# Decoding the last two matrices in the later two passes, in the buffers of h; the tail's buffers laid out anew

## The chip, the cores and the metric

The kernel runs on one core of one Trainium2 chip. The time is device microseconds (us) of one execution. Engines: TensorE (PE, its weight loads PEld), VectorE (DVE), ScalarE (ACT), GpSimd (POOL) and SyncE (SP), which issues the DMA transfers. Each engine works through its own instructions in order.

## What is computed

Three blocks follow each other on 2304 tokens (4 batches of 576) of width 512. All weights are inputs; `w_in` and `w_out` are 64-bit floats that the kernel turns into 32-bit ones itself ("decoding"), since it takes them as raw words.

```python
x = block_causal_attention(q, k, v)          # 4 x 8 heads, 576 x 64, blocks of 64
P = sinkhorn(exp(x @ w_gate), 8 rounds)      # 2304 x 8
out = 0
for e in range(8):                           # all experts, weighted by P
    out += P[:, e:e + 1] * (relu(x @ w1[e]) @ w2[e])
h = out @ w_in                               # 2304 x 1024
solu = h * softmax(h)
ln = layernorm(solu) * g_ln
return ln @ w_out                            # 2304 x 512
```

## The kernel before, in words

Every 32-bit product is made of three products of a high and a low part, so each operand is split: ScalarE casts the high part, GpSimd or VectorE subtracts it to get the low part (`split_weights`, lines 526 to 529).

**Expert layers.** Expert 0 runs between the pieces of attention. Experts 1 to 7 are 14 "units" (half an expert each, u = 2 to 15) and go over the tokens in three passes of two blocks of 384. The first layer uses seven products instead of eight (`first_layer`, L798 to L800 in `product`); VectorE forms the sums between them (`plus`, L810).

- Pass 0 (tokens 0 to 767) also makes the factors of all weights: `first_factors` and `second_weights` split them on ScalarE and GpSimd and write them to DRAM (`fd`). The second layer is plain (`second_layer`, L953 to L955), and VectorE adds each product times its gate (L959): six accumulations in a unit.
- Passes 1 and 2 read the factors back (`W<-fd`, a ring of 20 tiles in pool `wr`, 14 tiles in a unit). VectorE weights h with the gate (L852) into tiles of pool `hb` (8 tiles); `steps` forms the seven sums and splits of h: ScalarE casts (L859), GpSimd subtracts (L860) and makes differences (`minus`, L863; one of the four on VectorE). The second layer has 14 products a unit, one unit behind the first layer, and VectorE accumulates them (L907). `finish_pass` joins the sums at a pass's end and writes rows to DRAM (`rd`).

**Decoding.** `decode` (L536) handles half a row block of `w_in` or `w_out`: a 256 KB load, seven VectorE operations on 128x256 (L548 to L566; an eighth for `w_out`, L568), the split by ScalarE (L528) and GpSimd (L529), and a store to DRAM (`wd`). There are 32 of them. Two tiles of 4 KB a partition in a pool of their own, `wdp`, hold the words and the result. `late_decode(n)` issues those due at step n; the list `when` asks for 6 in pass 0 and 26 in passes 1 and 2.

**Tail.** After pass 2, for each of 18 row blocks: `early` loads x and transposes or copies it, `front` multiplies by `w_in` into two double banks (pool `big`) and normalises, `turn` transposes, `back` multiplies by `w_out`. `early` for two row blocks is issued ahead of `finish_pass(2)`, the others two steps ahead of their `front`.

**What sets the order.** The code names the work in one sequence; a scheduler puts each engine's instructions in order, by priority (place in the sequence) and by when buffers and inputs are free in its own estimate. Work whose buffers are free can stand earlier on an engine than the source has it. A tile waits for the release of what lay in its place, also across pools that take turns in one address range (`left` and `right` ends of the memory).

Of the kernel before, what the change touches and what calls it, by code (L numbers as in the profile page):

```python
# [19 lines left out]
P = 128  # L20
# [7 lines left out]
def build(ctx, tc, qT, kT, v, w_gate, w1, w1s, w2, w_in, w_out, g_ln, out):  # L28
# [509 lines left out]
    def decode(i, half, src, scale=None):  # L538


        pair = wdp.tile([P, 2, 512], F32R, tag="wd", name="w64")
        raw = pair[:, 0, :].bitcast(U32)
# [26 lines left out]
        t = pair[:, 1, :].rearrange("p (s n) -> p s n", s=2)  # L569
# [451 lines left out]
    l1p = lctx.enter_context(tc.tile_pool(name="l1p", bufs=6, space=PSUM, side="right"))  # L1021
    rctx = ExitStack()
    xcp = rctx.enter_context(tc.tile_pool(name="xcp", bufs=1, side="right"))
    xraw = rctx.enter_context(tc.tile_pool(name="xraw", bufs=1, side="right"))
    wdp = rctx.enter_context(tc.tile_pool(name="wdp", bufs=2, side="right"))
    wr = rctx.enter_context(tc.tile_pool(name="wr", bufs=20, side="right"))
    sctx = ExitStack()
    sml = sctx.enter_context(tc.tile_pool(name="sml", bufs=4, side="right"))
    stg2 = sctx.enter_context(tc.tile_pool(name="stg2", bufs=2, side="right"))
    jnk = sctx.enter_context(tc.tile_pool(name="jnk", bufs=1, side="right"))  # L1030
# [42 lines left out]
    when = sorted([*range(8, 27), *range(30, 42), 36])  # L1073
# [8 lines left out]
    for u in range(2, 16):  # L1082
        hs = {}
        first_layer(W, X, plain_hidden(hs))
        if u < 15:
            W, nws = first_factors(u + 1, raws[0]), second_weights(u + 1, raws[1])
            if u < 14:
                raws = fetch_first(u + 2), fetch_second(u + 2)
        else:
            X = {}  # L1090
            run(spread_x(1, X))
            W = load_factors(2, 0)
        late_decode(u - 2)
        if u == 4:
            gate_table()
        second_layer(u, 0, ws, hs)
        ws = nws
# [7 lines left out]
    hb = ectx.enter_context(tc.tile_pool(name="hb", bufs=8, side="left"))  # L1105
# [3 lines left out]
    for n, (p, u) in enumerate([*work, (3, 2)]):  # L1109
        if n < len(work):  # L1110
# [5 lines left out]
            late_decode(n + 14)  # L1116
# [16 lines left out]
    xin = ctx.enter_context(tc.tile_pool(name="xin", bufs=2, side="right"))  # L1133
    w2p = ctx.enter_context(tc.tile_pool(name="w2p", bufs=8, side="right"))
    wi = [[load_decoded(wip, 2 * dc + f) for f in range(2)] for dc in range(4)]
    early0 = [xin.tile([P, DM], F32, tag="x", name="xin") for t in range(2)]
    for t in range(2):
        nc.sync.dma_start(early0[t], adram[:, t * DM : t * DM + DM])
    def early(t):
        x2 = w2p.tile([P, 2, 4, P], F32R, tag="w", name="x2")  # L1140
        if t < 2:
# [3 lines left out]
        if t < 6:  # L1145
            if t > 1:
# [11 lines left out]
    xs = [early(t) for t in range(2)]  # L1158
# [5 lines left out]
    wop = ctx.enter_context(tc.tile_pool(name="wop", bufs=8, side="left"))  # L1164
    wo = [load_decoded(wop, 8 + c) for c in range(8)]


    mp = ctx.enter_context(tc.tile_pool(name="mp", bufs=3, side="left"))
# [70 lines left out]
    for i in range(NT + 4):  # L1239
        if i + 2 < NT:  # L1240
# [52 lines left out]
```

## Time and profile before

| what | value |
|---|---|
| median of 3 runs | 1988.7 us (1988.07 to 1994.13) |
| the profiled execution | 1991.78 us, its span 1990.0 us |
| busy share of the span: PE, DVE, ACT, POOL | 93%, 75%, 43%, 55% |
| DMA | 300.47 MB, mean 151 GB/s |
| mean granted clock of TensorE | 0.973 |

The span runs from the first to the last instruction; a busy share over all of it mixes stages that have different limits. The granted clock is 1.00 at 2.4 GHz and 0.5 at 1.2 GHz; a value between is a mean over time at either.

### The profile page before, as it was taken

How to read it: one execution, taken by the hardware profiler on the slowest of the kernel's cores; microseconds unless marked ns; L12 is line 12 of the kernel's file. 1: busy time of each engine (PE TensorE's matmuls, PEld its weight loads, DVE VectorE, ACT ScalarE, POOL GpSimd, SP SyncE). 2: the span in 40 equal slices, each digit the busy share in tenths (PEclk: the TensorE clock that was granted, in tenths of full speed). 3: DMA queues.
4: the chain of work that ended last, by engine and by line, in shares of the span. 5: the costliest groups of instructions: out<-in, count | busy, mean ns of one | idle time of the engine just before them, and what ended most of it. 6: DMA issues, size and time to landing. Idle time of an engine off the chain costs nothing.

```text
span 1990.0 us, 31023 instructions
## 1 busy us (share of the span) xinstructions
PE 1843.5 (93%) x10548; PEld 1229.7 (62%) x10548; DVE 1501.5 (75%) x3295; ACT 849.2 (43%) x1639; POOL 1086.0 (55%) x914
## 2 busy tenths in 40 slices
PE   5799999887888888989999999999899999989999
PEld 4688988785443444445566666665566666668887
DVE  6878777678998999777657766789577667778774
ACT  5676656564554555565242222232322222224332
POOL 7665646256564555575285556667765566631000
PEclk8999999998899999999999999999999999989999
DMA  8665554344665656555554554546445445541100
GB/s 228 158 173 151 158 148 125 139 139 157 216 214 172 216 180 200 192 196 172 162 148 145 143 144 140 146 142 187 145 142 145 142 140 147 166 173 43 45 31 32
DMA packets 191710, 300.47 MB, mean 151 GB/s; under 512 B 19760, under 2 KB 77760, under 8 KB 189632
## 3 DMA queue, kind: packets, MB, share of 16 engines
q1 hardware_dynamic: 191552, 298.49, 49.8%
q8 instruction: 84, 1.38, 0.3%
q14 instruction: 74, 0.61, 0.1%
HBM read 192.96 MB, written 77.14 MB: 136 GB/s over the span
## 4 chain that ended last, share of the span: by engine, by line
PE 51%; DVE 10%; DMA 3%; issue 2%; POOL 2%; ACT 1%; SPq 0%; POOLq 0%; ACTq 0%; DVEq 0%
PE yps L800 6%; PE yps L799 6%; PE yps L798 6%; PE psb L798 3%; PE psb L799 3%; PE psb L800 3%; PE psc L798 2%; PE psc L799 2%; PE psc L800 2%; PE psa L800 2%; PE psa L799 2%; PE psa L798 2%; PE ops L1230 2%; PE ops L1231 2%; PE ops L1232 2%
## 5 line engine op out<-in xcount | busy, mean ns | idle before, releaser
L860 POOL TENSOR_TENSOR hf<-hb,hf 128x768 f16<-128x768 f32 x196 | 324.0, 1667 | 242.9 <-ACT hf L859 242.8
L859 ACT CAST hf<-hb 128x768 f16<-128x768 f32 x196 | 159.8, 831 | 419.2 <-POOL hb L863 200.3
L799 PEld LDWEIGHTS <-W 128*128 128x128 f16 x1960 | 193.6, 99 | 170.1 <-issue 45.4
L907 DVE SCALAR_TENSOR_TENSOR acc<-yps,rscw,acc 128x384 f32<-128x384 f32 x364 | 220.7, 615 | 85.5 <-PE yps L800 84.0
L798 PEld LDWEIGHTS <-W 128*128 128x128 f16 x1960 | 193.8, 99 | 141.7 <-ACT W L528 10.2
L800 PEld LDWEIGHTS <-W 128*128 128x128 f16 x1960 | 194.0, 99 | 132.2 <-issue 4.9
L798 PE MATMUL yps<-hf,W 128*128 128x384 f16 x784 | 255.9, 327 | 4.8 <-ACT acc L905 4.5
L799 PE MATMUL yps<-hf,W 128*128 128x384 f16 x784 | 256.2, 327 | 0.0
L800 PE MATMUL yps<-hf,W 128*128 128x384 f16 x784 | 255.5, 327 | 0.0
L798 PE MATMUL psb<-X,W 128*128 128x384 f16 x504 | 166.7, 331 | 27.7 <-DVE u L810 16.5
L863 POOL TENSOR_TENSOR hb<-hb 128x768 f32<-128x768 f32 x84 | 153.4, 1827 | 24.3 <-DVE hb L852 22.3
L799 PE MATMUL psb<-X,W 128*128 128x384 f16 x504 | 166.5, 330 | 0.0
L800 PE MATMUL psb<-X,W 128*128 128x384 f16 x504 | 166.0, 330 | 0.0
L810 DVE TENSOR_TENSOR u<-psb,r 128x384 f32<-128x384 f32 x168 | 92.3, 551 | 88.2 <-PE psb L800 80.4
L953 PE MATMUL yps<-w,h 128*128 128x512 f16 x336 | 132.3, 394 | 27.4 <-DVE acc L959 24.3
L529 POOL TENSOR_TENSOR w<-raw,w 128x512 f16<-128x512 f32 (+1 forms) x96 | 119.9, 1266 | 46.0 <-ACT w L528 45.6
L245 POOL TENSOR_SCALAR e<-e,sv 128x128 f32<-128x128 f32 (+2 forms) x144 | 82.8, 577 | 98.4 <-DVE sv L241 37.7
L529 POOL TENSOR_TENSOR W<-raw,W 128x512 f16<-128x512 f32 x84 | 106.4, 1282 | 51.0 <-ACT W L528 47.1
L954 PE MATMUL yps<-w,h 128*128 128x512 f16 x336 | 132.2, 394 | 0.0
L955 PE MATMUL yps<-w,h 128*128 128x512 f16 x336 | 131.3, 391 | 0.0
L1214 POOL TENSOR_SCALAR lh<-ln 128x1024 f16<-128x1024 f32 x18 | 18.8, 1046 | 188.7 <-DVE sm L1186 86.1
L798 PE MATMUL psa<-X,W 128*128 128x384 f16 x336 | 111.7, 332 | 6.5 <-ACT W L528 4.9
(258 smaller groups left out, 4728.5 us busy)
## 6 DMA issues: line engine op xcount, KB each, us to landing
W<-fd SPq DMA_DIRECT2D x392, 256.0 KB, 2.7
fd<-W SPq DMA_DIRECT2D x154, 256.0 KB, 2.2
raw<-in_w1s SPq DMA_DIRECT2D x14, 1024.0 KB, 5.9
raw<-in_w SPq DMA_DIRECT2D x14, 1024.0 KB, 6.2
fd<-w SPq DMA_DIRECT2D x84, 128.0 KB, 2.2
raw<-in_w SPq DMA_DIRECT2D x40, 256.0 KB, 3.4
kh<-khigh SPq DMA_DIRECT2D x64, 144.0 KB, 2.6
kl<-kraw SPq DMA_DIRECT2D x64, 144.0 KB, 2.7
```

The lines of the kernel that those rows point to most:

```text
L529: nc.gpsimd.tensor_tensor(t[:, 1, :], raw, full(t[:, 0, :]), op=ALU.subtract)
L798: nc.tensor.matmul(ps, wh, xl, start=start and kc == 0, stop=False, skip_group_check=True)
L799: nc.tensor.matmul(ps, wh, xh, start=False, stop=False, skip_group_check=True)
L800: nc.tensor.matmul(ps, wl, xh, start=False, stop=stop and kc == 1, skip_group_check=True)
L810: nc.vector.tensor_tensor(to, bank[g, a], tmp[g, "r1" if a == "b" else name[1:]], op=ALU.add)
L859: nc.scalar.copy(hi, a)
L860: nc.gpsimd.tensor_tensor(lo, a, hi, op=ALU.subtract)
L863: eng.tensor_tensor(o, a, b, op=ALU.subtract)
L907: nc.vector.scalar_tensor_tensor(a, ps, r, a, op0=ALU.mult, op1=ALU.add)
L953: nc.tensor.matmul(ps, hl, ws[c][:, 0, :], start=c == 0, stop=False)
L954: nc.tensor.matmul(ps, hh, ws[c][:, 1, :], start=False, stop=False)
L955: nc.tensor.matmul(ps, hh, ws[c][:, 0, :], start=False, stop=c == 3)
```

## The change

The two tiles of a decoding now come from `hb`, the ring of h's tiles in passes 1 and 2, which grows from 8 to 10 tiles; the pool `wdp` goes. The list `when` now holds only steps of passes 1 and 2 (n = 0 to 26, with two decodings at 4, 8, 18, 22 and 24), and pass 0 no longer calls `late_decode`.

In the tail, x has four tiles (`xin`) below the pools of the passes, the first four row blocks are loaded into them once pass 0's sums are in DRAM, and `early` for three row blocks is issued ahead of `finish_pass(2)`. Its results have a pool of their own (`x2p`), the small buffers (`mp`) lie on the other side, and a tile without use (`gap`) sets the distance between pools.

```diff
     def decode(i, half, src, scale=None):
-        pair = wdp.tile([P, 2, 512], F32R, tag="wd", name="w64")
-        raw = pair[:, 0, :].bitcast(U32)
+        raw, t = (hb.tile([P, 2, BLK], F32, tag="hb", name=f"w{i}") for i in ("64", "32"))
+        raw, t = (a.rearrange("p k n -> p (k n)")[:, 0:512] for a in (raw, t))
+        raw = raw.bitcast(U32)
...
-        t = pair[:, 1, :].rearrange("p (s n) -> p s n", s=2)
+        t = t.bitcast(F32R).rearrange("p (s n) -> p s n", s=2)
         split_weights(t, f)
...
+    xin = ctx.enter_context(tc.tile_pool(name="xin", bufs=4, side="right"))
     rctx = ExitStack()
...
-    wdp = rctx.enter_context(tc.tile_pool(name="wdp", bufs=2, side="right"))
+    rctx.enter_context(tc.tile_pool(name="gap", bufs=1, side="right")).tile([P, 1792], F32, name="gap")
+    sml = rctx.enter_context(tc.tile_pool(name="sml", bufs=4, side="right"))
+    jnk = rctx.enter_context(tc.tile_pool(name="jnk", bufs=1, side="right"))
     wr = rctx.enter_context(tc.tile_pool(name="wr", bufs=20, side="right"))
...
-    when = sorted([*range(8, 27), *range(30, 42), 36])
+    when = sorted([*range(27), 4, 8, 18, 22, 24])
...
-        late_decode(u - 2)
         if u == 4:
             gate_table()
...
-    hb = ectx.enter_context(tc.tile_pool(name="hb", bufs=8, side="left"))
+    hb = ectx.enter_context(tc.tile_pool(name="hb", bufs=10, side="left"))
...
-            late_decode(n + 14)
+            late_decode(n)
...
-    xin = ctx.enter_context(tc.tile_pool(name="xin", bufs=2, side="right"))
-    w2p = ctx.enter_context(tc.tile_pool(name="w2p", bufs=8, side="right"))
+    x2p = ctx.enter_context(tc.tile_pool(name="x2p", bufs=3, side="right"))
+    mp = ctx.enter_context(tc.tile_pool(name="mp", bufs=3, side="right"))
...
-    early0 = [xin.tile([P, DM], F32, tag="x", name="xin") for t in range(2)]
-    for t in range(2):
+    early0 = [xin.tile([P, DM], F32, tag="x", name="xin") for t in range(4)]
+    for t in range(4):
         nc.sync.dma_start(early0[t], adram[:, t * DM : t * DM + DM])
...
-    xs = [early(t) for t in range(2)]
+    xs = [early(t) for t in range(3)]
     finish_pass(2)
...
+    w2p = ctx.enter_context(tc.tile_pool(name="w2p", bufs=6, side="left"))
...
-    mp = ctx.enter_context(tc.tile_pool(name="mp", bufs=3, side="left"))
...
-        if i + 2 < NT:
+        if 0 < i < NT - 2:
             xs.append(early(order[i + 2]))
```

Most lines behind the first edit move by one, so L959 of before is L960 of the change.

VectorE in pass 0, unit u = 5, from the first accumulation (`acc<-yps`) on. Here `psc`, `psb` are sums of the first layer, `raw` and `s` the factors, `h` the low parts of h, `a`, `b`, `f` (and `w`) a decoding. Before:

```order
L959 SCALAR_TENSOR_TENSOR acc<-yps,prw,acc 128x512 x2
L810 TENSOR_TENSOR psc<-psc,u_7152 128x384
L560 ISA a_13152<-a_13152,b_13153 128x512
L751 TENSOR_TENSOR raw<-s_7261,raw 128x512
L784 TENSOR_TENSOR s_7312<-raw_7024 128x512
L810 TENSOR_TENSOR psc<-psc,u_7161 128x384
L562 TENSOR_SCALAR b_13153<-w_13150 128x256
L566 SCALAR_TENSOR_TENSOR f_13160<-b_13153,a_13152 128x256
L959 SCALAR_TENSOR_TENSOR acc<-yps,prw,acc 128x512
L757 TENSOR_TENSOR raw<-raw 128x512
L841 SCALAR_TENSOR_TENSOR h<-psb,h 128x384
L548 TENSOR_SCALAR a_13457<-w_13455 128x256
```

The same place in the change, to the sixth accumulation of the unit:

```order
L960 SCALAR_TENSOR_TENSOR acc<-yps,prw,acc 128x512
L752 TENSOR_TENSOR raw<-s_7265,raw 128x512
L785 TENSOR_TENSOR s_7316<-raw_7028 128x512
L960 SCALAR_TENSOR_TENSOR acc<-yps,prw,acc 128x512
L811 TENSOR_TENSOR psc<-psc,u_7156 128x384
L811 TENSOR_TENSOR psc<-psc,u_7165 128x384
L758 TENSOR_TENSOR raw<-raw 128x512
L842 SCALAR_TENSOR_TENSOR h<-psb,h 128x384
L960 SCALAR_TENSOR_TENSOR acc<-yps,prw,acc 128x512
L842 SCALAR_TENSOR_TENSOR h<-psb,h 128x384
L842 SCALAR_TENSOR_TENSOR h<-psc,h 128x384 x2
L960 SCALAR_TENSOR_TENSOR acc<-yps,prw,acc 128x512 x3
```

Before, operations of two decodings stand among the accumulations of this unit; in the change there is none in any unit of pass 0.

VectorE in a steady unit of pass 1, the accumulations of the second layer. Before:

```order
L907 SCALAR_TENSOR_TENSOR acc<-yps,rscw,acc 128x384
L852 SCALAR_TENSOR_TENSOR hb<-psc,pb 128x384
L907 SCALAR_TENSOR_TENSOR acc<-yps,rscw,acc 128x384
L907 SCALAR_TENSOR_TENSOR acc_10396<-yps,rscw,acc_10396 128x384 x6
L907 SCALAR_TENSOR_TENSOR acc<-yps,rscw,acc 128x384 x4
L863 TENSOR_TENSOR hb<-hb 128x768
```

In the change, a unit with one decoding:

```order
L908 SCALAR_TENSOR_TENSOR acc<-yps,rscw,acc 128x384 x2
L549 TENSOR_SCALAR a_10940<-w_10937 128x256
L558 TENSOR_SCALAR b_10941<-w_10937 128x256
L908 SCALAR_TENSOR_TENSOR acc_10308<-yps,rscw,acc_10308 128x384
L552 SCALAR_TENSOR_TENSOR a_10940<-w_10937,a_10940 128x256
L908 SCALAR_TENSOR_TENSOR acc_10308<-yps,rscw,acc_10308 128x384
L555 SCALAR_TENSOR_TENSOR a_10940<-w_10937,a_10940 128x256
L908 SCALAR_TENSOR_TENSOR acc_10308<-yps,rscw,acc_10308 128x384
L561 ISA a_10940<-a_10940,b_10941 128x512
L908 SCALAR_TENSOR_TENSOR acc_10308<-yps,rscw,acc_10308 128x384
L563 TENSOR_SCALAR b_10941<-w_10937 128x256
L567 SCALAR_TENSOR_TENSOR f_10948<-b_10941,a_10940 128x256
```

The decoding's operations stand between the accumulations, one by one; six more accumulations follow.

GpSimd in the same pass: splits (`hf`), differences (`hb`) and, in the change, the decoding's subtraction (`w<-f`). Before, one unit:

```order
L860 TENSOR_TENSOR hf<-hb,hf 128x768 x6
L863 TENSOR_TENSOR hb<-hb 128x768 x2
L860 TENSOR_TENSOR hf<-hb,hf 128x768
L863 TENSOR_TENSOR hb<-hb 128x768
L860 TENSOR_TENSOR hf<-hb,hf 128x768 x6
```

In the change:

```order
L861 TENSOR_TENSOR hf<-hb,hf 128x768 x6
L864 TENSOR_TENSOR hb<-hb 128x768
L529 TENSOR_TENSOR w_11242<-f_11252,w_11242 128x256
L864 TENSOR_TENSOR hb<-hb 128x768
L861 TENSOR_TENSOR hf<-hb,hf 128x768
L864 TENSOR_TENSOR hb<-hb 128x768
L861 TENSOR_TENSOR hf<-hb,hf 128x768 x6
```

The subtraction of the decoding stands between the first two differences of a unit.

## Rows read from the trace of the kernel before

**Rows 1.** Busy us of each engine by stretch (x instructions), granted clock, DMA share, GB/s.

```profile
459.00:811.00 352.00, 285.36 (x1392) 141.95 (x1391) 325.56 (x614) 188.81 (x314) 204.03 (x168) 0.91 0.62 199
811.00:985.00 174.00, 167.76 (x892) 87.08 (x891) 126.81 (x238) 92.17 (x150) 91.40 (x76) 1.00 0.52 170
1046.00:1319.00 273.00, 273.00 (x1682) 164.38 (x1681) 192.43 (x331) 65.82 (x90) 167.41 (x100) 1.00 0.51 143
1319.00:1441.00 122.00, 112.72 (x670) 66.20 (x669) 97.69 (x140) 41.01 (x64) 92.21 (x53) 0.97 0.54 163
```

The columns behind the length are PE, PEld, DVE, ACT, POOL.

**Rows 2.** One line of the decoding: ns min/median/max, first and last start.

```profile
L551 DVE SCALAR_TENSOR_TENSOR a<-w,a x32: 406/418/1376, 461.4 to 808.2; 128x256 uint32<-128x256 uint32 x32
```

**Rows 3.** Groups by line, 459 to 818 us: count | busy us, mean ns | idle before.

```profile
L557 DVE TENSOR_SCALAR b<-w 128x256 uint32<-128x256 uint32 x32 | 24.7, 772 | 0.0
L551 DVE SCALAR_TENSOR_TENSOR a<-w,a 128x256 uint32<-128x256 uint32 x32 | 23.5, 735 | 0.0
L554 DVE SCALAR_TENSOR_TENSOR a<-w,a 128x256 uint32<-128x256 uint32 x32 | 22.2, 693 | 0.3
L566 DVE SCALAR_TENSOR_TENSOR f<-b,a 128x256 f32<-128x256 uint32 x32 | 20.7, 648 | 1.0
L562 DVE TENSOR_SCALAR b<-w 128x256 uint32<-128x256 uint32 x32 | 19.9, 623 | 0.3
L548 DVE TENSOR_SCALAR a<-w 128x256 uint32<-128x256 uint32 x32 | 19.9, 622 | 12.6 <-DMA w<-in_w_out 6.4 <-DMA w<-in_w_in 6.1
L560 DVE CUSTOM_DVE_ANT_0 a<-a,b 128x512 uint16<-128x512 uint16 x32 | 18.6, 582 | 0.2
L568 DVE TENSOR_SCALAR f<-f,gsc 128x256 f32<-128x256 f32 x16 | 9.3, 580 | 0.2
L529 POOL TENSOR_TENSOR w<-f,w 128x256 fp32r<-128x256 f32 x32 | 27.0, 842 | 67.6 <-ACT w L528 67.6
L528 ACT CAST w<-f 128x256 fp32r<-128x256 f32 x32 | 12.8, 400 | 51.5 <-DVE f L566 20.4 <-issue 19.2 <-DVE f L568 4.9
```

**Rows 4.** Waits of TensorE, 459 to 811 us: us in total, times, longest.

```profile
PE yps L953 <- DVE acc L959: 18.6, 13, 3.7
PE psb L798 <- DVE u L810: 15.2, 7, 6.6
PE tot L454 <- DVE acc L959: 10.5, 6, 3.4
PE psa L798 <- ACT W L528: 4.9, 3, 2.2
```

**Rows 5.** Accumulations of pass 1 by stretch: DVE busy (x instructions), clock, DMA share, GB/s.

```profile
1046.00:1319.00 273.00, 85.45 (x140) 1.00 0.51 143
```

**Rows 6.** Timeline of VectorE: start us, length us.

```profile
613.44 1.37 DVE L551 SCALAR_TENSOR_TENSOR a<-w,a 128x256 uint32<-128x256 uint32 x1
```

**Rows 7.** Timeline of GpSimd at the same time.

```profile
613.33 5.09 POOL L529 TENSOR_TENSOR w<-raw,w 128x512 f16<-128x512 f32 x4
```

**Rows 8.** Groups by line, 1046 to 1319 us.

```profile
L860 POOL TENSOR_TENSOR hf<-hb,hf 128x768 f16<-128x768 f32 x70 | 114.2, 1643 | 96.1 <-ACT hf L859 96.1
L863 POOL TENSOR_TENSOR hb<-hb 128x768 f32<-128x768 f32 x30 | 54.4, 1813 | 9.3 <-DVE hb L852 8.5
```

**Rows 9.** Timeline of VectorE at the start of the tail [idle before].

```profile
1759.04 5.38 DVE L941 SCALAR_TENSOR_TENSOR acc<-y,cpi,acc 128x768 f32<-128x768 f32 x4
...
1774.13 2.35 DVE L1181 TENSOR_REDUCE nm<-h 128x1 f32<-128x1024 f32 x2
```

**Rows 10.** Timeline of TensorE at the start of the tail.

```profile
1770.17 1.29 PE L1150 MATMUL xtp<-ident,xin 128*128 128x128 f32 x8 [2.65 <-DMA xin<-ad]
1775.47 1.94 PE L1150 MATMUL xtp<-ident,xin 128*128 128x128 f32 x8 [4.01 <-DVE nm L1181]
1778.57 0.77 PE L1177 MATMUL h<-w,x 128*128 128x512 f32 x1 [1.16 <-DVE sm L1186]
```

More of the change, by code (lines that the diff above doesn't have):

```diff
@@ L1024, in build @@
     xraw = rctx.enter_context(tc.tile_pool(name="xraw", bufs=1, side="right"))
-    wdp = rctx.enter_context(tc.tile_pool(name="wdp", bufs=2, side="right"))
+    rctx.enter_context(tc.tile_pool(name="gap", bufs=1, side="right")).tile([P, 1792], F32, name="gap")
+    sml = rctx.enter_context(tc.tile_pool(name="sml", bufs=4, side="right"))
+    jnk = rctx.enter_context(tc.tile_pool(name="jnk", bufs=1, side="right"))
     wr = rctx.enter_context(tc.tile_pool(name="wr", bufs=20, side="right"))
     sctx = ExitStack()
-    sml = sctx.enter_context(tc.tile_pool(name="sml", bufs=4, side="right"))
     stg2 = sctx.enter_context(tc.tile_pool(name="stg2", bufs=2, side="right"))
-    jnk = sctx.enter_context(tc.tile_pool(name="jnk", bufs=1, side="right"))
     ones = const.tile([P, P], F32, name="ones")
@@ L1132, in build @@
     wip = ctx.enter_context(tc.tile_pool(name="wip", bufs=8, side="right"))
-    xin = ctx.enter_context(tc.tile_pool(name="xin", bufs=2, side="right"))
-    w2p = ctx.enter_context(tc.tile_pool(name="w2p", bufs=8, side="right"))
+    x2p = ctx.enter_context(tc.tile_pool(name="x2p", bufs=3, side="right"))
+    mp = ctx.enter_context(tc.tile_pool(name="mp", bufs=3, side="right"))
     wi = [[load_decoded(wip, 2 * dc + f) for f in range(2)] for dc in range(4)]
-    early0 = [xin.tile([P, DM], F32, tag="x", name="xin") for t in range(2)]
-    for t in range(2):
+    early0 = [xin.tile([P, DM], F32, tag="x", name="xin") for t in range(4)]
+    for t in range(4):
         nc.sync.dma_start(early0[t], adram[:, t * DM : t * DM + DM])
     def early(t):
-        x2 = w2p.tile([P, 2, 4, P], F32R, tag="w", name="x2")
-        if t < 2:
+        x2 = x2p.tile([P, 2, 4, P], F32R, tag="x2", name="x2")
+        if t < 4:
             x = early0[t]
@@ L1145, in early @@
         if t < 6:
-            if t > 1:
+            if t > 3:
                 nc.sync.dma_start(x, adram[:, t * DM : t * DM + DM])
```

## The prediction

> **What bounds the kernel now.** I read the busy times by stretch first. Pass 0 of the expert layers begins near 459 us and its 14 units end at 985 us. In passes 1 and 2 TensorE is busy all the time at the full granted clock, while pass 0 falls in two halves that do the same kind of work [rows 1]. From 459 to 811 us VectorE is busy 325.56 of 352 us, and TensorE only 285.36 at a mean granted clock of 0.91. From 811 to 985 us VectorE is at 126.81 of 174 us, and TensorE at 167.76 at 1.00. The reader is to see that the bound changes inside one pass, at 811 us.
>
> What stops at 811 us is the decoding. The 32 decodings (seven VectorE operations each, eight for `w_out`) all start between 461 and 808 us [rows 2], although the source asks for 26 of them in passes 1 and 2: the scheduler pulled them forward, since nothing but the two buffers of `wdp` held them back. They cost 24.7 + 23.5 + 22.2 + 20.7 + 19.9 + 19.9 + 18.6 + 9.3 = 158.8 us of VectorE, 4.96 us each [rows 3]. That is nearly half of its busy time in that stretch.
>
> The waits of TensorE there are for VectorE: 18.6 us for a bank that the accumulation has not emptied, 15.2 us for `plus`, 10.5 us ahead of `total` [rows 4]. These rows say that in the first half of pass 0 taking VectorE work away is worth TensorE time, which a share of busy time over the whole span (75% for VectorE) would hide.
>
> **What the change moves, and what it is worth in pass 0.** A decoding now needs two tiles of `hb`, a pool that is opened after pass 0. So none can be pulled forward, and the order shows the accumulations of unit 5 with no decoding among them, where before pieces of two stood. I take pass 0 without decodings to run as its second half did. That half did 892 matmuls in 174 us, 5.13 per us; at that pace the 1392 matmuls of the first half [rows 1] take 271.5 us instead of 352, a gain of 80.5 us. I count by matmuls and not by units, since at 811 us TensorE stands in the middle of later units' first layers. I take off 6 us for what the second half does not have: the gate table in unit 4 and the first unit, which waits for its weights on ScalarE (waits on `W` L528 are 4.9 us in [rows 4], and I leave most of them in place). So the term is **-74 us**. Its bounds: at most 90 us, if the pace were that of no stop at all (167.76 us for the 892 give 262 for the 1392); at least half of it, 37 us, if another chain takes over (first rival). VectorE itself would not: its 325.56 us less the 158.8 are 167 us in 271.
>
> **What the decodings cost in passes 1 and 2.** A steady unit there has 14 accumulations; 140 in 273 us make ten units of 27.3 us [rows 5], with 192.43 / 10 = 19.2 us of VectorE [rows 1]. So VectorE has 8.1 us to spare in each. The 27 units from n = 0 to 26 take 22 single decodings and 5 double ones. At 4.96 us a single fits (24.2 of 27.3). A double needs 9.9 and overruns by 1.8 us, which the 3.1 us left in the next unit take up. In between, banks of PSUM are the buffer: the product pool and `mm` hold eight, and an accumulation is due every 0.98 us (27.3 / 28 products).
>
> Is 4.96 us the right price there? One decoding operation took 406 ns at least, 418 in the middle, 1376 at most [rows 2]. The long ones stand beside GpSimd: the 1.37 us operation at 613.44 [rows 6] began as GpSimd started four subtractions in a row that fill 613.33 to 618.42, 1.27 us each [rows 7], and it ended just after the first of them. So the price is set by GpSimd's operation in flight. In passes 1 and 2 GpSimd is busy 167.41 of 273 us (61%, against 58% in 459 to 811), with operations of 1643 and 1813 ns [rows 1, 8]. From below, no operation meets GpSimd: 7.5 x 0.41 = 3 us a decoding. From above, every one waits behind one: the 1.3 us of the long cases plus the 0.4 to 0.5 us by which GpSimd's operations are longer, 1.8 x 7.5 = 13.5 us. I stay near 5, because the order puts a cushion in: on GpSimd the decoding's own subtraction (L529) stands after the first `minus` of a unit, and on ScalarE its cast stands before the third cast of h's tiles. GpSimd therefore stops there until f is done, and while it stops VectorE's decoding runs free of it.
>
> That stop is the wait that the change adds. Behind the subtraction on GpSimd stand two `minus` and five splits of the unit, about 2 x 1.81 + 5 x 1.64 = 11.8 us. GpSimd's work per unit is 16.7 us and 0.84 for the decoding, so it can lose 9 us in each unit before it is late. For whom: R's splits are used by the products one unit later. ScalarE's copy of `r1` stands behind the late casts; at most 1 to 2 us, and VectorE then is still busy with accumulations.
>
> Two places have no such slack. At the change from pass 1 to 2, 1319 to 1441 us, VectorE already fills 97.69 of 122 us and TensorE loses 9 us; the four decodings of those units add 20 us to a slack of 24. And at the start of pass 1 seven decoding operations stand in a row ahead of the next `plus`. I price them at 6 and 2 us: **+8 us**. Bounds: 0, and the rival below.
>
> The new SyncE work is the same 64 transfers, moved. SyncE waits in order for a tile of `hb` and for the subtraction, and W's loads stand behind; they run through a ring of 20 tiles with 14 used in 27.3 us, so about 39 us ahead, and a wait of 8 us there is hidden. The tenth and ninth tile of `hb` pay for the two that a decoding holds.
>
> **The tail.** Before, VectorE ended the last gated sums at 1759.04 + 5.38 = 1764.42 and then took the first row maximum only at 1774.13 [rows 9]: in its order rows 2 and 3 of x stood ahead, and these were issued behind loads of the weights, landing for TensorE at 1770.17. TensorE stood still for 2.65, 4.01 and 1.16 us and began the third front at 1778.57 [rows 10], 4.44 us after the maximum began. Now the four rows come in during pass 1, three are turned before the last pass is finished, the constant and the small buffers lie on the other side, and nothing stands between the sums and the maximum. The third front can begin at 1764.42 + 4.44 = 1768.9: **-10 us** (-9.7). It is at least the 4 us of the longest stop, and at most 12. The last front rows and their outputs are untouched.
>
> **Sum.** The profiled execution took 1991.78 us: 1991.78 - 74 + 8 - 10 = 1915.8. It is 3.1 us over the median of the runs, 1988.7; on that scale 1912.7, so **1913 us**.
>
> **The rivals.**
> *Another chain holds pass 0.* Without decodings ScalarE and GpSimd still have the factors of each unit: ScalarE 188.81 - 12.8 and GpSimd 204.03 - 27.0 us [rows 1, 3], each 65% of 271. Against: the second half of pass 0 has the same factors in most of its units, and TensorE is idle there for 6.2 of 174 us. If half the gain were lost: 1913 + 37 = 1950.
>
> *The decodings meet GpSimd in passes 1 and 2, and VectorE is the bound there.* For it: with 24.2 of 27.3 us VectorE is 89% full, and TensorE has no slack at all to give. If every second operation meets GpSimd (1.8 and 0.41 us, 8.3 us a decoding), singles overrun by 0.2 and doubles by 8.5: 22 x 0.2 + 5 x 8.5 = 47 us, 1913 + 47 = 1960. It ends on the other side when a decoding costs 9.2 us: 22 x 1.1 + 5 x 10.3 = 76 us, with the 8 just the 84 gained. At 13.5 us it would be 22 x 5.4 + 5 x 18.9 = 213, and 2126 in all. Against it stands the cushion above.
> The Trainium skill says (SBUF — State Buffer, "SBUF: two separate sides") that VectorE and GpSimd share a port pair as an exclusive lock, held for the whole instruction, so the loser blocks fully. By that rule the 13.5 us hold wherever GpSimd runs back to back, and the sum would be 2126; the 1.37 us operation beside GpSimd agrees with the rule, the median of 418 ns shows how seldom it bites.
>
> *Nothing moves.* The pool could let decodings back into pass 0; the order shows the first after the last accumulation of pass 0. Then only the tail would count: 1979.
>
> **Chances.** Forecast 0.66, first rival 0.14, the second at about 1960 0.10 and past its turning point 0.05, nothing moves 0.05. The range reaches from the upper bounds of both gains without a cost (1988.7 - 90 - 12 = 1887, taken as 1885) up to the first rival, 1950, which leaves out 2 in 10; the forecast's own is 1885 to 1930. A measurement of this kernel tells 0.3%, some 6 us, from no change: faster 0.92, same 0.03, slower 0.05.
>
> **What would show it.** Right: no decoding before 985 us; VectorE under 75% and TensorE's clock near 1.00 from 459 to the end of pass 0, which comes about 74 us earlier; units of 27.3 us in passes 1 and 2 with decoding operations near 0.66 us on average; TensorE's stop after the second front under 2 us. Wrong: accumulations in passes 1 and 2 that TensorE waits for in the double units, decodings of 8 us or more, a clock under 1.00 there, or waits on `W` L528 that grow in pass 0.

## The result and the profile after

The change takes 1938.56 us (median of 4 runs, 1933.8 to 1941.58) against 1989.24 us of the kernel before on the same chip, a ratio of 0.9738 with a 95% interval of 0.9711 to 0.9766. The forecast was 1913 us: the direction and the order of size are right, 25 us of the gain are missing. The profiled execution took 1940.68 us with a span of 1938.9 us; the mean granted clock of TensorE rose from 0.973 to 0.982.

To see where the 51 us came from and where 25 more went, I cut both spans at the last accumulation of each unit (VectorE's L959 and L907 of before, L960 and L908 of the change) and compare the pieces. All lengths are us of the profiled execution.

| stretch | before | after | difference | forecast |
|---|---|---|---|---|
| start to the end of pass 0 | 984.2 | 919.3 | -64.9 | -74 |
| first unit of pass 1 | 35.5 | 41.4 | +5.9 | +2 |
| 11 further units of pass 1 | 299.1 | 302.7 | +3.6 | 0 |
| three units around the change from pass 1 to 2 | 95.7 | 106.9 | +11.2 | +6 |
| 12 units of pass 2 | 327.2 | 330.3 | +3.1 | 0 |
| last unit | 13.7 | 15.8 | +2.1 | 0 |
| tail, to its last computing instruction | 231.4 | 219.4 | -12.0 | -10 |

Both spans run on for 3.1 us behind the last row. The three terms of the sum are thus -65, +26 and -12, where -74, +8 and -10 stood. The busy times by stretch (columns as in [rows 1]) answer to those of before: pass 0, eleven units of pass 1, the change of passes, twelve units of pass 2.

```profile
456.00:919.00 463.00, 431.40 (x2300) 226.57 (x2299) 324.75 (x614) 269.69 (x432) 255.88 (x211) 0.98 0.54 180
961.00:1263.00 302.00, 301.34 (x1853) 181.11 (x1852) 243.74 (x454) 74.29 (x111) 193.98 (x122) 1.00 0.55 163
1263.00:1370.00 107.00, 89.66 (x500) 50.41 (x498) 87.08 (x131) 35.38 (x59) 80.46 (x48) 0.92 0.54 169
1370.00:1700.00 330.00, 328.71 (x2017) 197.26 (x2016) 276.03 (x508) 83.51 (x125) 220.46 (x138) 1.00 0.53 165
```

In pass 0 VectorE is at 70% (324.75 of 463) and the clock at 0.98, where the first half had 0.91 [rows 1]. From 459 to 811 us TensorE now does 1715 matmuls, 4.87 per us where the working took 5.13, and is still idle for 30.6 of the 352 us. In the steady units TensorE is idle for 2 of 632 us although VectorE works at 81 to 84%: the decodings fit there. TensorE is idle in the third row, 17 of 107 us.

One line of the decoding (as [rows 2]):

```profile
L552 DVE SCALAR_TENSOR_TENSOR a<-w,a x32: 406/414/2024, 933.3 to 1667.8; 128x256 uint32<-128x256 uint32 x32
```

No decoding stands before 919 us, and a steady unit takes 27.5 us (302.7 / 11) where it took 27.2. The groups by line of the decoding from 919 to 1720 us (as [rows 3]), in the order of their work L549, L558, L552, L555, L561, L563, L567, L569, and the subtraction on GpSimd:

```profile
L558 DVE TENSOR_SCALAR b<-w 128x256 uint32<-128x256 uint32 x32 | 24.0, 750 | 0.0
L549 DVE TENSOR_SCALAR a<-w 128x256 uint32<-128x256 uint32 x32 | 22.0, 686 | 8.4 <-DMA w<-in_w_out 5.1 <-DMA w<-in_w_in 3.3
L555 DVE SCALAR_TENSOR_TENSOR a<-w,a 128x256 uint32<-128x256 uint32 x32 | 19.2, 601 | 0.1
L552 DVE SCALAR_TENSOR_TENSOR a<-w,a 128x256 uint32<-128x256 uint32 x32 | 17.4, 545 | 0.0
L567 DVE SCALAR_TENSOR_TENSOR f<-b,a 128x256 f32<-128x256 uint32 x32 | 13.3, 416 | 0.8
L561 DVE CUSTOM_DVE_ANT_0 a<-a,b 128x512 uint16<-128x512 uint16 x32 | 13.2, 413 | 0.2
L563 DVE TENSOR_SCALAR b<-w 128x256 uint32<-128x256 uint32 x32 | 9.1, 284 | 0.3
L569 DVE TENSOR_SCALAR f<-f,gsc 128x256 f32<-128x256 f32 x16 | 5.5, 343 | 0.1
L529 POOL TENSOR_TENSOR w<-f,w 128x256 fp32r<-128x256 f32 x32 | 24.2, 755 | 174.9 <-ACT w L528 169.0 <-DMA W<-fd 5.9
```

The first eight sum to 123.7 us, 3.87 a decoding, below the 4.96 of the forecast. Two things are to be read here. The first four operations are long (545 to 750 ns), the last four short (284 to 416): GpSimd runs beside the first and has stopped by the time of the last. And the last row tells where it stopped: 169.0 us, 5.3 us a decoding, in front of the decoding's own subtraction, for ScalarE's cast of f. This is the cushion of the prediction, and also the wait that the change adds.

The waits of TensorE in pass 0 (as [rows 4]); the long list of waits for accumulations and sums is gone, and one stop is new:

```profile
PE yps L954 <- DVE t L459: 9.6, 1, 9.6
PE yps L954 <- DVE acc L960: 5.8, 5, 2.6
PE yps L954 <- DVE h L842: 5.2, 2, 2.7
```

Its chain is followed back through the timelines of TensorE, ScalarE and SyncE (start, length, in brackets the idle time before and what ended it):

```profile
683.07 0.59 PE L954 MATMUL yps<-w,h 128*128 128x512 f16 x1 [9.63 <-DVE t L459]
```

```profile
678.33 1.91 ACT L480 ACTIVATE junk<-raw 128x2048 bf16<-128x2048 f32 x1 [8.37 <-DMA raw<-in_w1s]
```

```profile
657.66 11.38 SPq L744 DMA_DIRECT2D fd<-W  x7
669.14 0.38 SPq L725 DMA_DIRECT2D raw<-in_w1s  x1
```

SyncE stands from 657.66 in seven stores of factors that wait for GpSimd's subtractions; the load of the next raw weights stands behind them and goes out at 669.14. ScalarE waits for it 8.37 us, and behind that wait stand, on ScalarE, TensorE and VectorE, the square sum and the operation `t` (L459) that releases TensorE.

The waits of TensorE from 919 to 1370 us, from the start of pass 1 past its change to pass 2:

```profile
PE yps L799 <- POOL hf L861: 11.9, 2, 6.6
PE yps L799 <- DVE hb L853: 5.6, 5, 2.3
```

The 11.9 us are two stops, one at the start of each pass. The timelines of VectorE, ScalarE, GpSimd and TensorE there:

```profile
932.89 0.29 DVE L549 TENSOR_SCALAR a<-w 128x256 uint32<-128x256 uint32 x1 [1.52 <-DMA w<-in_w_in]
...
936.74 0.55 DVE L811 TENSOR_TENSOR vu<-psc,u 128x384 f32<-128x384 f32 x1
...
945.74 1.73 DVE L558 TENSOR_SCALAR b<-w 128x256 uint32<-128x256 uint32 x1
947.39 2.02 DVE L552 SCALAR_TENSOR_TENSOR a<-w,a 128x256 uint32<-128x256 uint32 x1
...
1357.17 0.51 DVE L549 TENSOR_SCALAR a<-w 128x256 uint32<-128x256 uint32 x1 [5.13 <-DMA w<-in_w_out]
```

```profile
935.46 0.41 ACT L528 CAST w<-f 128x256 fp32r<-128x256 f32 x1 [9.02 <-DVE f L567]
```

```profile
935.95 0.73 POOL L529 TENSOR_TENSOR w<-f,w 128x256 fp32r<-128x256 f32 x1 [7.58 <-ACT w L528]
936.63 1.82 POOL L864 TENSOR_TENSOR hb<-hb 128x768 f32<-128x768 f32 x1
...
947.28 1.85 POOL L864 TENSOR_TENSOR hb<-hb 128x768 f32<-128x768 f32 x1
951.76 0.88 POOL L529 TENSOR_TENSOR w<-f,w 128x256 fp32r<-128x256 f32 x1 [2.63 <-ACT w L528]
...
1361.48 0.72 POOL L529 TENSOR_TENSOR w<-f,w 128x256 fp32r<-128x256 f32 x1 [3.96 <-ACT w L528]
```

```profile
956.05 0.48 PE L799 MATMUL yps<-hf,W 128*128 128x384 f16 x1 [5.32 <-POOL hf L861]
...
1365.62 0.48 PE L799 MATMUL yps<-hf,W 128*128 128x384 f16 x1 [6.58 <-POOL hf L861]
```

The first decoding of pass 1 begins late (its words land after VectorE has been idle 1.52 us), ScalarE stands 9.02 us for f and GpSimd 7.58 us behind ScalarE; the second decoding costs GpSimd 2.63 us more. These 10.2 us come where the second layer has just begun and no split of R lies in store. At 956.05 TensorE has used up what was there and has stood for 5.32 us. The change of passes repeats it: words late by 5.13 us, GpSimd stopped for 3.96, TensorE for 6.58.

Why the first words of pass 1 come so late is told by SyncE's queue. The four loads of rows of x, which belong to the tail's half of the change, wait there for pass 0's sums to reach DRAM, and the load of the words stands behind them:

```profile
926.29 1.37 SPq L1139 DMA_DIRECT2D xin<-ad  x3
927.71 0.43 SPq L544 DMA_DIRECT2D w<-in_w_in  x1
```

The tail, VectorE and TensorE (as [rows 9, 10]):

```profile
1719.90 3.52 DVE L942 SCALAR_TENSOR_TENSOR acc<-y,cpi,acc 128x768 f32<-128x768 f32 x2
1723.35 0.68 DVE L1156 TENSOR_TENSOR x<-xtp,x 128x512 fp32r<-128x512 f32 x1
1723.95 1.93 DVE L942 SCALAR_TENSOR_TENSOR acc<-y,cpi,acc 128x768 f32<-128x768 f32 x2
1725.80 1.21 DVE L1182 TENSOR_REDUCE nm<-h 128x1 f32<-128x1024 f32 x1
```

```profile
1730.11 0.47 PE L1178 MATMUL h<-w,x 128*128 128x512 f32 x1 [0.82 <-DVE e L1190]
```

The row maximum follows the sums at once, and the third front begins 4.31 us behind it (4.44 in the working), after a stop of 0.82 us.

### The profile page after: what moved, and what is told of

It reads as the page before. It is cut to its first block, busy times and chain, and to the rows that moved or that the text cites. A ratio compares the mean times of both kernels' runs of the same rounds, so it can differ in the third digit from the quotient of the medians.

```text
span 1938.9 us, 31098 instructions
## 1 busy us (share of the span) xinstructions
PE 1823.0 (94%) x10548; PEld 1223.2 (63%) x10548; DVE 1469.3 (76%) x3295; ACT 843.1 (43%) x1639; POOL 1077.7 (56%) x914
## 4 chain that ended last, share of the span: by engine, by line
PE 51%; DVE 15%; POOL 12%; issue 11%; DMA 7%; ACT 3%; SPq 1%; POOLq 0%; ACTq 0%; DVEq 0%
POOL hb L864 4%; POOL hf L861 4%; PE yps L799 3%; PE yps L800 3%; PE yps L801 3%; DMA raw<-in_w1s 2%; PE psb L799 2%; PE psb L801 2%; PE psb L800 2%; DVE acc L908 2%; PE av L303 2%; PE yps L954 2%; PE ops L1231 2%; PE ops L1233 2%; PE yps L955 2%
## 5 line engine op out<-in xcount | busy, mean ns | idle before, releaser
L861 POOL TENSOR_TENSOR hf<-hb,hf 128x768 f16<-128x768 f32 x196 | 329.9, 1705 | 80.4 <-ACT hf L860 76.6
L799 PE MATMUL yps<-hf,W 128*128 128x384 f16 x784 | 257.2, 329 | 17.6 <-POOL hf L861 11.9
L908 DVE SCALAR_TENSOR_TENSOR acc<-yps,rscw,acc 128x384 f32<-128x384 f32 x364 | 211.8, 606 | 3.8 <-PE yps L801 3.6
L529 POOL TENSOR_TENSOR w<-raw,w 128x512 f16<-128x512 f32 (+1 forms) x96 | 118.7, 1254 | 94.0 <-ACT w L528 85.9
L954 PE MATMUL yps<-w,h 128*128 128x512 f16 x336 | 129.3, 386 | 21.6 <-DVE t L459 9.6
L955 PE MATMUL yps<-w,h 128*128 128x512 f16 x336 | 129.4, 385 | 0.0
L956 PE MATMUL yps<-w,h 128*128 128x512 f16 x336 | 129.2, 385 | 0.0
L529 POOL TENSOR_TENSOR W<-raw,W 128x512 f16<-128x512 f32 x84 | 98.0, 1185 | 47.8 <-ACT W L528 42.9
L528 ACT CAST w<-f 128x256 fp32r<-128x256 f32 x32 | 13.0, 405 | 253.8 <-DVE f L567 115.3
L529 POOL TENSOR_TENSOR w<-f,w 128x256 fp32r<-128x256 f32 x32 | 24.2, 755 | 174.9 <-ACT w L528 169.0
```

The lines of the kernel that those rows point to most:

```text
L529: nc.gpsimd.tensor_tensor(t[:, 1, :], raw, full(t[:, 0, :]), op=ALU.subtract)
L799: nc.tensor.matmul(ps, wh, xl, start=start and kc == 0, stop=False, skip_group_check=True)
L861: nc.gpsimd.tensor_tensor(lo, a, hi, op=ALU.subtract)
L908: nc.vector.scalar_tensor_tensor(a, ps, r, a, op0=ALU.mult, op1=ALU.add)
L954: nc.tensor.matmul(ps, hl, ws[c][:, 0, :], start=c == 0, stop=False)
L955: nc.tensor.matmul(ps, hh, ws[c][:, 1, :], start=False, stop=False)
```

## The experiments

Lengths of stretches are cut as in the table above. The two halves of the change come first.

**The tail alone.** The decodings stay in their own pool and in pass 0.

```diff
-        raw, t = (hb.tile([P, 2, BLK], F32, tag="hb", name=f"w{i}") for i in ("64", "32"))
+        pair = wdp.tile([P, 2, 512], F32R, tag="wd", name="w64")
...
-    when = sorted([*range(27), 4, 8, 18, 22, 24])
+    when = sorted([*range(8, 27), *range(30, 42), 36])
```

> Decodings and their list as before, in the pool wdp; the tail as in the change (one tile less in W's ring, for room). If the tail is worth what its stretch shows (from the last accumulation of pass 2 to the end 234.5 us before, 222.6 after), it is 12 us faster than before: 1977 us. If the rows of x that are loaded early only moved a wait, or pass 0 gained from the new layout, it is within 4 us of before, or more than 20 us faster.

1975.26 us, ratio 0.9938 (0.9918 to 0.9958), 11.6 us less than the 1986.83 of before, measured beside it, as expected. Its tail takes 219.4 us, the same as in the full change.

**The decodings alone.** The tail is the old one.

```diff
-    xs = [early(t) for t in range(3)]
+    xs = [early(t) for t in range(2)]
...
-        if 0 < i < NT - 2:
+        if i + 2 < NT:
```

> The tail as before, decodings in hb in passes 1 and 2. By the sum of stretches: 65 us gained in pass 0, 26 given back in passes 1 and 2, so 39 us faster than before, 1950 us. If the two parts lean on each other (the early rows hide something in the passes, or the late decodings delay the tail's weights), it differs from 1950 by more than 5 us.

1951.24 us, ratio 0.9817 (0.9796 to 0.9838): -35.6 us. The two halves sum to -47.2 us; the full change gave -50.7, and in intervals of this width that is the same. The stretches do not add up in that way, though: the halves lean on each other twice. (The profiled execution is the longest of this version's four, 1956.89 us.)

At the start of pass 1 no load of x stands ahead of the words. They land for VectorE 10.2 us behind the end of pass 0, in the change 13.6. GpSimd stops for 5.04 us at the first decoding and not at all at the second, TensorE does not stop, and the first unit takes 34.5 us, with the same decodings in it that go with 41.4 us in the change (35.5 before). TensorE's mean granted clock there is 1.00, in the change 0.92.

```profile
932.22 0.73 POOL L529 TENSOR_TENSOR w<-f,w 128x256 fp32r<-128x256 f32 x1 [5.04 <-ACT w L528]
```

At the start of the old tail TensorE then stands much longer for the rows of x than before (2.65 us, [rows 10]), and the tail takes 243.5 us instead of 231.4:

```profile
1722.16 1.94 PE L1149 MATMUL xtp<-ident,xin 128*128 128x128 f32 x8 [15.27 <-DMA xin<-ad]
```

So the passes cost 19.2 us here and not 26, and the time came near the expected 1950 us by two differences that offset each other.

**The pool or the list?** The new list, but a pool of its own, open from the start.

```diff
-        raw, t = (hb.tile([P, 2, BLK], F32, tag="hb", name=f"w{i}") for i in ("64", "32"))
+        pair = wdp.tile([P, 2, 512], F32R, tag="wd", name="w64")
...
-    hb = ectx.enter_context(tc.tile_pool(name="hb", bufs=10, side="left"))
+    hb = ectx.enter_context(tc.tile_pool(name="hb", bufs=8, side="left"))
```

> Everything as in the change, the new list of units for the decodings too, but their two tiles come from a pool of their own that is open from the start, as before the change. If the pool decides where the decodings run: all of them in the first half of pass 0 again, 1975 us as only_tail. If the list decides: 1939 us.

1976.46 us, ratio 0.994 (0.9925 to 0.9956). The view of one line shows all 32 in the first half of pass 0 again:

```profile
L551 DVE SCALAR_TENSOR_TENSOR a<-w,a x32: 406/418/1379, 460.5 to 806.4; 128x256 uint32<-128x256 uint32 x32
```

The list of steps does nothing by itself; what keeps a decoding back is that its tiles don't exist before.

**Starts without decodings, all others doubled.** None at n = 0, 1, 13, 14, 15.

```diff
-    when = sorted([*range(27), 4, 8, 18, 22, 24])
+    when = sorted([*range(2, 13), *range(16, 27), 4, 6, 8, 10, 12, 18, 20, 22, 24, 26])
```

> As the change, but no decoding in the first two units of pass 1 and the last and first two of passes 1 and 2 (n = 0, 1, 13, 14, 15); ten units take two instead of five. If the price in the passes is paid at their starts, where GpSimd waits for a decoding while TensorE needs its splits soon, some 6 us come back at the first and 8 to 10 at the second: 1923 to 1927 us. If it is paid everywhere, by VectorE's load and by waits behind GpSimd, the five more double units cost as much as they give back: 1938 us or more.

1936.09 us, ratio 0.9742 (0.9721 to 0.9764): no gain. But the stretches tell more than the time: the first unit fell from 41.4 to 33.8 us and the change of passes from 106.9 to 100.3, 14.2 us in all, while the units with the added doubles of pass 1 cost 5.6 us and the last unit, behind the double at n = 26, 7.9 us. So in the layout of the change the starts do pay for their decodings, and a double is not free either.

**The subtraction on VectorE,** so that GpSimd has no part in a decoding.

```diff
-        split_weights(t, f)
+        nc.scalar.copy(t[:, 0, :], f)
+        nc.vector.tensor_tensor(t[:, 1, :], f, full(t[:, 0, :]), op=ALU.subtract)
```

> As the change, but the decoding's subtraction is made by VectorE, so that GpSimd never waits for a decoding. If GpSimd's wait for f is the cause at the starts of the passes, the two waits of TensorE for hf (5.3 and 6.6 us) go: 1927 us. If VectorE's load is the cause, it has 32 operations more (0.4 to 1.5 us each, 13 to 48 us in all) and the time is 1940 us or more.

1942.23 us, ratio 0.9779 (0.9757 to 0.9801): missed, it is no faster. The passes take 805.3 us, 8.3 more than in the change (pass 0 ends 6.6 us earlier), and TensorE still stands 12.0 us for `hf` between 900 and 1370 us. The timelines of ScalarE and GpSimd at the first decoding show why:

```profile
928.99 0.40 ACT L571 CAST w<-f 128x256 fp32r<-128x256 f32 x1 [9.12 <-DVE f L567]
```

```profile
930.75 1.65 POOL L862 TENSOR_TENSOR hf<-hb,hf 128x768 f16<-128x768 f32 x1 [7.08 <-ACT hf L861]
```

ScalarE still stands 9.12 us for f, and the casts of h that GpSimd needs stand behind it. The stop of GpSimd has another name and nearly its old length (7.08 us for 7.58).

**Both parts of the split one step later,** so that f is long done when ScalarE and GpSimd come to it. For this f has four buffers, and the result's tile is taken a step later.

```diff
+        yield
+        t = hb.tile([P, 2, BLK], F32, tag="hb", name="w32").rearrange("p k n -> p (k n)")[:, 0:512]
         split_weights(t, f)
...
-        for i, w in enumerate(when):
-            if w == n:
-                decode(*late[i])
+        jobs = [decode(*late[i]) for i, w in enumerate(when) if w == n]
+        for job in open_splits + jobs:
+            next(job, None)
+        open_splits[:] = jobs
```

> As the change, but the cast and the subtraction of a decoding are issued one step later, so that f is long done when ScalarE and GpSimd come to them. The run with the subtraction on VectorE kept the waits of TensorE for hf, and ScalarE's cast of f still stood ahead of the casts of h there. If the in-order wait for f, on ScalarE as much as on GpSimd, is what the starts of the passes pay, the first unit of pass 1 comes down from 41.4 to some 35.5 us and the change of passes from 107 to some 100: 1926 us. If VectorE's own load is what they pay, nothing moves: 1938 us. The decoding's last operations, which run free of GpSimd in the change (284 to 416 ns), should then meet GpSimd again, in either case.

1968.13 us, ratio 0.9901 (0.9886 to 0.9916): 30 us slower than the change. Three groups of the decoding:

```profile
L557 DVE TENSOR_SCALAR b<-w 128x256 uint32<-128x256 uint32 x32 | 46.6, 1455 | 0.0
L551 DVE SCALAR_TENSOR_TENSOR a<-w,a 128x256 uint32<-128x256 uint32 x32 | 41.5, 1297 | 0.0
L562 DVE TENSOR_SCALAR b<-w 128x256 uint32<-128x256 uint32 x32 | 32.4, 1011 | 0.1
```

All eight sum to 256.7 us, 8.02 a decoding instead of 3.87: GpSimd no longer stops for a decoding (0.0 us idle ahead of L529), and 164 of VectorE's 240 operations take over a quarter longer than the shortest of their kind (43 in the change). The passes take 827.6 us (797.0 in the change): 33.7 more in the 23 steady units, 3.2 less in the first unit. TensorE now waits for accumulations:

```profile
PE psa L800 <- DVE acc L909: 28.7, 24, 1.8
```

This is the second rival's mechanism (1960 us at 8.3 us a decoding), brought about by taking the cushion away.

**One operation instead of seven.** It leaves out six of VectorE's seven operations, so the words don't become the right numbers; loads, casts, subtractions and stores stay.

```diff
-        nc.vector.tensor_scalar(
-            a, hi, 3, 0x3FFFFFFF, op0=ALU.logical_shift_left, op1=ALU.bitwise_and
-        )
...
+            f.bitcast(U32), hi, 3, 0x3FFFFFFF, op0=ALU.logical_shift_left, op1=ALU.bitwise_and
```

> As the change, with one VectorE operation in place of seven in each decoding (the words are not turned into the right numbers; the loads, the split, the scaling by g and the stores stay). It takes some 100 us of VectorE work out of passes 1 and 2 and makes f early. If VectorE's part is what the passes pay (26 us more than before in passes 1 and 2), nearly all of it comes back: 1915 us. If the split on ScalarE and GpSimd, the stores or the tiles of hb are, at most 5 us come back: 1933 us.

1915.97 us, ratio 0.9636 (0.9618 to 0.9653). The passes take 771.3 us, before the change 771.2. So without the six operations the 26 us are gone; tiles, transfers, casts and subtractions cost nothing that shows. GpSimd still stops for the first decoding, whose words are as late, but less, and not at the second:

```profile
934.35 0.73 POOL L529 TENSOR_TENSOR w<-f,w 128x256 fp32r<-128x256 f32 x1 [4.62 <-ACT w L528]
...
947.47 1.45 POOL L529 TENSOR_TENSOR w<-f,w 128x256 fp32r<-128x256 f32 x1
```

At the start of pass 1 a stop of 4.62 us cost TensorE nothing, nor did the 5.04 us of the decodings alone; 10.2 us cost it 5.32.

**The seven operations twice** (same result, twice the work of VectorE).

```diff
+        for _ in range(2):
+            nc.vector.tensor_scalar(
+                a, hi, 3, 0x3FFFFFFF, op0=ALU.logical_shift_left, op1=ALU.bitwise_and
+            )
...
```

> As the change, with the seven operations of each decoding done twice (the result is the same). Measured, a decoding takes 3.9 us of VectorE in passes 1 and 2 and a unit has 8.1 us to spare: twice the work needs some 7 us, which a single unit still has, and 14 us in five double ones, over by 6. So 30 to 40 us from the double units, and more at the starts of the passes as f comes later there (10 to 15 us): 1980 us. If the passes pay for every operation on VectorE, the 123 us of more work come on top: 2060 us. If they only pay at the starts, 1950 us.

2020.12 us, ratio 1.0156 (1.0139 to 1.0173), 40 us over what I expected. The decoding's operations took 262.8 us of VectorE, 139 more than in the change, and the passes 880.4, 83 more. The waits of TensorE from 910 to 1400 us name GpSimd first, then VectorE:

```profile
PE yps L800 <- POOL hf L862: 15.8, 4, 8.5
PE yps L800 <- DVE hb L854: 13.0, 10, 2.8
```

I had counted only what no longer fits into VectorE's spare time; the stop of ScalarE and GpSimd for f grows with the decoding as well (214.4 us in all ahead of L529, 169.0 in the change).

**The raw loads of pass 0 issued by ScalarE,** so that they don't stand behind SyncE's stores.

```diff
-        nc.sync.dma_start(raw, w1s[e - 1, g])
+        nc.scalar.dma_start(raw, w1s[e - 1, g])
...
-        nc.sync.dma_start(raw, w2[e, 4 * g * P : (4 * g + 4) * P, :].rearrange("(c p) d -> p c d", p=P))
+        nc.scalar.dma_start(raw, w2[e, 4 * g * P : (4 * g + 4) * P, :].rearrange("(c p) d -> p c d", p=P))
```

> As the change, but the two 1 MB loads of a unit's raw weights in pass 0 are issued by ScalarE instead of SyncE. In the change TensorE stands still once for 9.6 us in pass 0, for the square sum of a raw weight whose load stood behind stores that waited for GpSimd in SyncE's queue. If that queue is the cause, the stop goes and pass 0 ends 6 to 9 us earlier: 1930 us. If the load is late because its buffer comes free late, or because of the other transfers, the stop stays: 1938 us.

1933.87 us, ratio 0.9725 (0.9711 to 0.974). The stop of 9.63 us is now one of 2.45:

```profile
674.00 0.38 PE L954 MATMUL yps<-w,h 128*128 128x512 f16 x1 [2.45 <-DVE t L459]
```

Another has grown from 0.7 to 4.03 us (at 561.14, for ScalarE's copy `r`). Pass 0 ends at 914.5 us, 4.8 earlier; 3.4 of these lie ahead of its first product (453.0 us, in the change 456.4), and from there it takes 461.5 us, in the change 462.9. That is no gain: six other runs here have pass 0 in the same order as the change on all four engines, and they take 460.4 to 464.3 us, with the same stop at 6.25 to 6.96 us (the 9.63 of the change is the longest of the seven). So the queue makes the stop, but taking it away did not make the pass shorter, and the intervals of the two ratios overlap.

**Decodings in the last two units of pass 0.** The second half of pass 0 left VectorE 47 us [rows 1]. The pool of raw words has nothing to load any more in the last two units, so its tiles can hold four or eight decodings. The raw loads are issued as in the run before.

```diff
-    when = sorted([*range(27), 4, 8, 18, 22, 24])
+    early_n = 8
+    when = [None] * early_n + sorted([*range(1, 13), *range(15, 27)])
...
+        if u >= 14:
+            for i in range((u - 14) * early_n // 2, (u - 13) * early_n // 2):
+                job = late[i]
+                decode(*job, **({} if len(job) > 3 else {"scale": None}), tag=("raw", "raw2")[i % 2])
```

(with four: `early_n = 4`, and doubles at 4, 8, 18 and 22.)

> Four of the 32 decodings go back into the last two units of pass 0 (in tiles of the pool of raw words, which are free by then), the others as in the change but none in the first unit of pass 1 nor in the two units at the change of passes; the two raw loads of pass 0 are issued by ScalarE as in act_load. If the passes pay for decodings where a pass starts: first unit 35.5 instead of 41.4 us, change of passes 99 instead of 107, the last units of pass 0 not longer by more than 2: about 1921 us. If the price is VectorE's total work wherever it lies: as act_load, 1934 us or more.

> As best4 with eight decodings in the last two units of pass 0 and no unit of passes 1 and 2 with two. VectorE has 38.98 of the last 58 us before the end of pass 0 in the kernel before, so about 19 us free; eight decodings ask 31 us at 3.87. If VectorE's free time there is the limit: pass 0 ends some 10 us later than in best4 and the passes gain at most 7: 1920 to 1926 us. If those units have more to give than that: 1915 us.

With four 1930.01 us, ratio 0.9713 (0.9695 to 0.9731); with eight 1926.41 us, ratio 0.969 (0.9672 to 0.9708). The version with eight beats the kernel before and the change (0.9711 to 0.9766). With four the expected 1921 us were missed: the first unit (36.2) and the change of passes (99.4) came down as expected, but pass 0 takes 472.3 us from its first product, 10.8 more than with the loads alone, where 2 had been allowed. With eight the stretches are: first unit 35.8 us, eleven units 299.3, change of passes 99.7, twelve units 328.4, last unit 13.7; the passes take 776.9 us in all, 5.7 over before, with 24 decodings in them. Two of the decoding's groups and GpSimd's first subtraction show the single decodings of this version:

```profile
L553 DVE TENSOR_SCALAR a<-w 128x256 uint32<-128x256 uint32 x24 | 22.5, 937 | 4.2 <-DMA w<-in_w_out 2.5 <-DMA w<-in_w_in 1.7
L559 DVE SCALAR_TENSOR_TENSOR a<-w,a 128x256 uint32<-128x256 uint32 x24 | 9.8, 410 | 0.1
```

```profile
955.68 0.72 POOL L529 TENSOR_TENSOR w<-f,w 128x256 fp32r<-128x256 f32 x1 [2.77 <-ACT w L528]
```

It is mainly the first operation that still meets GpSimd (937 ns); others take 410. Against this, pass 0 takes 470.2 us from its first product, 8.7 more than with the loads alone (461.5). That is no more than with four, where 10 us more had been expected, so the length of pass 0 does not go by the number of decodings in it; what sets it was not found.

**The early words loaded together.** In the version with eight, VectorE waited 6.7 us for words at the end of pass 0. Here the four loads of a unit go out ahead of its four decodings, into the two halves of both tiles.

```diff
+            for job, (raw, t) in zip(jobs, pairs):
+                nc.sync.dma_start(raw.bitcast(U32), job[2])
+            for job, pair in zip(jobs, pairs):
+                decode(*job, **({} if len(job) > 3 else {"scale": None}), tag=pair)
```

> As best8, but the words of the four decodings of a unit are loaded together, into the two halves of both tiles, ahead of the four decodings (in best8 each load waits until the decoding two places ahead has given its tile back, and VectorE waited 6.7 us for words at the end of pass 0). If these 6.7 us are what makes pass 0 end 8.7 us later in best8 than in act_load: some 5 us of them return, 1921 us. If the pass ends later for the VectorE work itself (30.4 us of decoding in the last units, accumulations behind it): no change from 1926 us.

1929.23 us, ratio 0.9701 (0.9687 to 0.9714): the same within the intervals. VectorE waited 5.8 us for words instead of 6.7, so this edit hardly moved the wait that it was to take away; whether the wait or the decodings' own work makes pass 0 take longer (472.6 us here) is not told apart by it.

## Why the prediction was right, and where it was off

**The mechanism held.** The bound of pass 0's first half was VectorE with the decodings; without them pass 0 is shorter by 65 us. The pool was what had let them in (the run with a pool kept). The first rival, another chain in pass 0 that takes half the gain, did not come; nor did the third.

**The term of -74 measured -65.** The step "I take pass 0 without decodings to run as its second half did" did not hold in full: the first half now runs at 4.87 matmuls per us, not 5.13, with 30.6 us of idle time on TensorE. One stop of 9.63 us, of the size of the difference, is a load that stands behind seven stores in SyncE's queue, which the prediction left out. That the stop comes from this queue is shown: with the loads issued by ScalarE it is 2.45 us. That the missing 9 us come from it is not shown: without the stop the pass was no shorter than in the runs that have it (461.5 us among 460.4 to 464.3). Their cause stays open.

**The term of +8 measured +26, and this is the step that failed.** It rested on two numbers: VectorE's spare time in a unit, and that GpSimd "can lose 9 us in each unit before it is late". In steady units both were right: the decodings cost +6.7 us over 23 units (3.6 and 3.1), and as singles, in the version with eight, +1.4 (0.2 and 1.2). At a pass's start the second was wrong, because there the splits of R are not one unit ahead: stops of 4.62 and 5.04 us on GpSimd were free, 10.2 us cost TensorE 5.32 us. For the start of pass 1 I had priced VectorE's seven operations at 2 us and not the stop of two other engines for their result; and I had priced the tail apart from the decodings, though its four loads of x stand ahead of the first words in SyncE's queue. Without them the first unit takes 34.5 us with its decodings, so they alone cost nothing there. (One profiled run shows this. That the later words make all of the difference is argued from the chain of waits, since the two kernels differ in the rest of the tail's layout too; rows of x loaded behind the first words were not run.) The change of passes, where I had seen the shortage, cost 11.2 us instead of 6 by the same chain, with the tail's half or without it (106.9 and 107.2 us).

**What showed the cause:** with six of seven operations left out the 26 us go; with no decodings in the starts the starts get their time back (33.8 and 100.3 us; 35.8 and 99.7 us, though the second of these versions differs in pass 0 too). The subtraction's place is not the cause (VectorE's variant), since ScalarE's cast stands in order too. How the cost of the starts divides between VectorE's time and ScalarE's stop was not separated: the one run that takes the stop away (both parts a step later) also doubles the price of the operations.

**The price of 4.96 us a decoding measured 3.87,** so the price was not what was too low. The cushion was right, and its worth is measured: without it 8.02 us a decoding and 30 us. The Trainium skill says (SBUF — State Buffer, "SBUF: two separate sides") that an operation of VectorE with two inputs in SBUF waits for the whole of a GpSimd operation that reads SBUF, if that one started first. The trace agrees: the operation at 947.39 began beside GpSimd's of 947.28 to 949.13 and took 2.02 us, ending 0.28 us behind it. But the wait falls only on the operations that meet GpSimd, and how many do is a matter of the order.

**The term of -10 measured -12,** alone -11.6, by its mechanism: third front 4.31 us behind the first maximum, stop 0.82 us. Part of what the early rows of x gain there is paid at the start of pass 1.

## What to carry to other kernels

Price work that is moved into a full stage by unit, and the first unit of a stage apart: an engine's slack in a steady unit comes from work that lies one unit ahead, and at a stage's start there is less of it (here 5.04 us of stops were free and 10.2 were not). Two edits that put work into the same queue are not priced apart: each half alone can look right in its total while the stretches shift. Where an in-order engine stops for a result, ask both what stands behind it and what runs free while it stops: here the stop was worth some 34 us in the 23 steady units (later split against the change) and went with 12 us of TensorE's waits at the starts. Where a list of steps and a pool both seem to set the order, look which of them the scheduler can't pass; here the list alone changed nothing while the pool stood open.

## What was not expected of the hardware

VectorE's `plus` was not slowed beside GpSimd: at 936.74 it took 0.55 us within GpSimd's 936.63 to 938.45, while the decoding's operations took up to 2.02. It reads one input from PSUM; the Trainium skill (the same section) says that an operation with at most one input in SBUF, outside VectorE's faster modes that use both ports, does not meet GpSimd, and this row agrees. The decoding's first operations have one input in SBUF and a constant, and were slowed nevertheless (L558 at 945.74: 1.73 us, and 0.28 at 1357.60 with GpSimd idle); which mode they ran in no row shows.
